# An even beat of loads, later weights and re-ordered row transposes in a gated linear attention followed by domain-routed experts

## The chip, the core and the metric

The kernel runs on one NeuronCore of a Trainium2 chip, in one launch. The metric is the device time of one execution in microseconds (us). TensorE does the matrix products, VectorE and ScalarE the elementwise work, GpSimd issues the indirect transfers and the weight loads, SyncE issues the loads of the inputs. Sixteen DMA engines serve all of them.

## The reference

Two parts, one after the other. The first is a recurrence over 768 time steps for 4 batches and 8 heads of 48 channels, with a complex decay per channel:

```python
mag = np.sqrt(a_re*a_re + a_im*a_im)
scale = np.minimum(mag, 0.999) / (mag + 1e-06)
a_re_n, a_im_n = a_re*scale, a_im*scale
for t in range(S):
    new_re = ar*S_re - ai*S_im
    new_im = ar*S_im + ai*S_re
    S_re, S_im = new_re + einsum('bhd,bhe->bhde', k[:,:,t], v[:,:,t]), new_im
    y[:,:,t] = einsum('bhd,bhde->bhe', q[:,:,t], S_re)
```

The second takes each of the 3072 tokens (4 x 768 rows of 384 numbers) through the one of 8 experts that its `domain_id` names:

```python
h = np.maximum(x[mask] @ w1[e], 0.0)     # 384 -> 1024
out[mask] = h @ w2[e]                    # 1024 -> 384
```

## The kernel before, in words

**Attention.** Each batch is cut into 6 chunks of 128 time steps, so there are 24 chunks, numbered g, and each chunk is worked in two halves of four heads: 48 steps, numbered s, step 2g and 2g+1 for chunk g. The decays of a batch are turned into logarithms and angles (`le_a`, `le_b`, `trig_a`), summed over time by matrix products with triangular masks (`sums`, L329), and made into factors by ScalarE (`le_c` writes the tile em, `trig_b` the tile sc). `prods(g)` (L344) multiplies k and q of chunk g into em on VectorE, `cat(g)` (L370) multiplies the sines and cosines in. Then `transposes(s)` (L382, copies L386 and L388), `scores(s)` (L394, masked on VectorE in L396), `state(g)` (L408), and `outputs(s)` (L422, L424), which writes rows of 384 numbers through the tile xst to a DRAM buffer for each batch, `gl_x_rows`.

**Experts.** `routing()` works out for each batch and expert which rows belong to it (up to 128), as lists of row numbers inv_sb. Each of the 32 pairs of batch and expert is one expert step: `gather` (L434, an indirect load of 128 rows of `gl_x_rows`, issued by GpSimd three steps ahead), `ffn_a` (three row transposes on TensorE, L442, and a copy on VectorE, L444), `ffn_b` (24 products and two ReLU copies, L456 and L458), `ffn_c` (8 products, a copy and an indirect store, L465 to L468). xt_ps of `ffn_a` and o_ps of `ffn_c` share one PSUM bank.

**Order.** The head prepares batch 0 and runs `routing`. Then a loop over s calls in each step `scores(s)`, the loads placed at this step, `outputs(s - 2)`, `transposes(s + 2)`, `state`, the preparation of the following batch (placed by `add`), and `expert_step(s)`. A framework then orders the instructions of each engine: it plays the program through with its own model of durations, and takes the earlier-written instruction where several are ready. So an instruction can come ahead of earlier-written ones on its engine if the model thinks that its inputs are there; a manual dependency (`add_manual_dep` with `nosync`) forbids that for a pair.

**Loads.** All input loads are one chain on SyncE's queue (`sp`, L122): the decays (576 KB each), k and q (two of 192 KB in one of six kq buffers) and v (192 KB in one of four vf buffers, cast to bf16 by `cast_v`, L119, at step 2g-3). One that waits for its buffer holds all behind it. The weights are 40 pieces, five for each expert, issued by GpSimd (L276, L279), each gated by the masking of the step at which `w_place(n)` puts it. An expert step is planned at the first free step that is three behind its last weight piece and at least 6 behind the end of its batch; steps 44 to 47 take none. What does not fit runs after step 47. Worked out from these formulas, before: weights end at step 35, expert steps are 18 to 20, 25, 29 to 40, 42, 43 and 48 to 61, so 14 of 32 lie behind the attention steps.

Of the kernel before, what the change touches and what calls it, by code (L numbers as in the profile page):

```python
# [25 lines left out]
NCH = S // TC  # L26
# [22 lines left out]
def kernel(  # L49
# [56 lines left out]
    def load_kq(g, which):  # L106
        if which == 0:
            kq_t[g] = lpool.tile([128, 2, H, D], F32, name="kq", bufs=6)
        sp(out=kq_t[g][:, which], in_=chunk_view((k, q)[which], g))
# [1 line left out]
    vf_t = {}  # L111

    def load_v(g):
        vf_t[g] = lpool.tile([128, H, D], F32, name="vf", bufs=4)
        sp(out=vf_t[g][:, :, :], in_=chunk_view(v, g))

    def cast_v(g):
# [14 lines left out]
    for g in range(NCH):  # L132
        load_kq(g, 0)
        load_kq(g, 1)
        if g < 4:
            load_v(g)


    def const(name, dt, val=1.0, cols=128):
# [202 lines left out]
    def prods(g):  # L342
        t = em[g // 2][:, :, g % 2]
        nc.vector.tensor_tensor(out=t, in0=kq_t[g][:, :, :, :].rearrange("p a h d -> p a (h d)"), in1=t, op=ALU.mult)  # L344
# [32 lines left out]
    def transposes(s):  # L377
# [10 lines left out]
        eng(out=flat(qt), in_=t_ps[0:96, 1].rearrange("p h t -> p (h t)"))  # L388
        kts[s], qts[s] = kt, qt

    def scores(s):
        s_ps = bank([128, 4, TC], F32, "s_ps", "s")
        for h in range(4):
            nc.tensor.matmul(out=s_ps[:, h, :], lhsT=kts[s][:, h, :], rhs=qts[s][:, h, :], start=True, stop=True)  # L394
        m = epool.tile([128, 4, TC], BF16, name="mtm", bufs=3)
        i = nc.vector.tensor_tensor(out=m[:, :, :], in0=s_ps[:, :, :],  # L396
                                    in1=mask[:, None, :].to_broadcast([128, 4, TC]), op=ALU.mult)
        mtms[s] = m
        return i
# [39 lines left out]
    def ffn_a(x):  # L439
        xt_ps = bank([128, 3, 128], F16, "xt_ps", "x")  # L440
        for fs in range(3):
            nc.tensor.transpose(out=xt_ps[:, fs, :], in_=x[:, fs * 128:(fs + 1) * 128], identity=ident16[:, :])  # L442
        xt = mpool.tile([128, 3, 128], F16, name="xt", bufs=2)
        nc.vector.tensor_copy(out=xt[:, :, :], in_=xt_ps[:, :, :])  # L444
        return xt
# [27 lines left out]

    def w_place(n):

        return n if n < 12 else 12 + (n - 12) * 3 // 2 if n < 20 else 24 + (n - 20) * 3 // 5

    preload = lambda name: chain("act", nc.scalar.preload_act_table_set(name))  # L478

# [3 lines left out]
    def add(s, f):  # L483
        steps[s].append(f)

    for b in range(1, B):
        s0 = 12 * (b - 1)
        g0 = b * NCH
        A, Z = (b, 0), (b, 1)
        add(s0 + 0, lambda: preload(SET_LE))  # L490
        add(s0 + 0, lambda A=A: le_a(A))
        add(s0 + 1, lambda Z=Z: le_a(Z))
        add(s0 + 1, lambda A=A: le_b(A))
        add(s0 + 2, lambda Z=Z: le_b(Z))
        for n, s in ((0, 2), (1, 3), (2, 4)):
            add(s0 + s, lambda p=g0 // 2 + n: le_c(p))
            add(s0 + s, lambda g=g0 + 2 * n: prods(g))
            add(s0 + s + 1, lambda g=g0 + 2 * n + 1: prods(g))
        add(s0 + 5, lambda: preload(SET_TRIG))
        add(s0 + 6, lambda A=A: trig_a(A))  # L500
        add(s0 + 6, lambda Z=Z: trig_a(Z))
        for n, s in ((0, 6), (1, 8), (2, 10)):
            add(s0 + s, lambda p=g0 // 2 + n: trig_b(p))

    for g in range(3, B * NCH):
        add(2 * g - 5, lambda g=g: cat(g))

    loads = {s: [] for s in range(NS)}
    for b in range(2, B):
        s0 = 12 * (b - 2)  # L510
        for hf in range(NH):
            loads[s0 + 3].append(lambda b=b, hf=hf: load_decay(b, hf, 0))
            loads[s0 + 7].append(lambda b=b, hf=hf: load_decay(b, hf, 1))
        for n in range(NCH):
            for w in range(2):
                loads[s0 + (3, 4, 5, 5, 8, 8)[n]].append(lambda g=b * NCH + n, w=w: load_kq(g, w))
    for g in range(6, B * NCH):
        loads[2 * g - 10].insert(0, lambda g=g: load_v(g))
    for g in range(3, B * NCH):
        add(2 * g - 3, lambda g=g: cast_v(g))  # L520

# [7 lines left out]
    left = [(b, e) for b in range(B) for e in range(NE)]  # L529
    s = 0  # L530
    while left:
        ready = [(b, e) for b, e in left if s >= 12 * (b + 1) + 6 and s >= w_slot[e] + WLAT]
        if ready and not NS - 4 <= s < NS:
            plan[s] = ready[0]
            left.remove(ready[0])
        s += 1
# [10 lines left out]
        load_decay(1, hf, 0)  # L547
    for n in range(3):
        le_c(n, (None, ("s", "x"), ("y", "h"))[n])
        prods(2 * n)  # L550
        prods(2 * n + 1)
        if n < 2:
            for g in range(2):
                load_kq(NCH + 2 * n + g, 0)
                load_kq(NCH + 2 * n + g, 1)
        if n == 0:
            routing()
    preload(SET_TRIG)
    trig_a(A)
    for g in range(3):  # L560
        cast_v(g)
    for g in range(4, 6):
        load_v(g)
    trig_a(Z)
    for hf in range(NH):
        load_decay(1, hf, 1)
    for g in range(4, 6):
        load_kq(NCH + g, 0)
        load_kq(NCH + g, 1)
    trig_b(0)  # L570
    cat(0)
    transposes(0)
# [2 lines left out]
    trig_b(1, ("x", "h"))  # L575
    cat(2)
    trig_b(2)
    xrows, xts, hs = {}, {}, {}
    order = [plan[s] for s in sorted(plan)]
    GA = 3  # L580
# [35 lines left out]
    def overflow():  # L616
        count = nc.values_load(ovf_i[0:1, 0:1], min_val=0, max_val=S)
        with tc.If(count > CAP):
# [5 lines left out]
            for b in range(B):  # L624
                with tc.For_i(0, NE, 1) as e:
# [8 lines left out]
                    for c in range(OVC):  # L634
                        ffn_c(ffn_b(ffn_a(gather(b, c, invo[:, c, 1:2])), w1o), w2o, invo[:, c, 0:1])

    overflow()


# [28 lines left out]
```

## Time and profile before

| what | us |
|---|---|
| median of 3 runs | 282.45 |
| lowest and highest run | 281.96 and 285.29 |
| profiled execution, its time | 280.33 |
| its span in the trace | 278.7 |
| TensorE busy in it | 211.2 (76%) |
| VectorE busy | 178.6 (64%) |
| ScalarE busy | 176.0 (63%) |
| GpSimd busy | 99.9 (36%) |

The trace covers the span; the time beside it has 1.6 us more around it. A busy share is an average over the whole span, and the stretches differ much, so the views below go by stretches.

### The profile page before, as it was taken

What the parts mean: (1) busy time and instruction counts of PE and PEld (TensorE: products, weight loads), DVE (VectorE), ACT (ScalarE), POOL (GpSimd) and SP (SyncE); (2) the same over time, 40 slices, a digit from 0 to 9 for tenths busy, and PEclk for the clock granted to TensorE, in tenths of its full rate; (3) what the DMA queues carried; (4) which work ended last, traced back from release to release, by engine and by line L of the source; (5) the groups of instructions that cost most, each with busy time, mean ns of one, the idle gap of its engine ahead of it and who ended that gap; (6) DMA issues with size and microseconds to landing.
All of it is one profiled execution on the core that took longest, in us unless ns stands there. A gap on an engine that the chain in (4) does not pass through costs nothing.

```text
span 278.7 us, 6242 instructions
## 1 busy us (share of the span) xinstructions
PE 211.2 (76%) x2450; PEld 164.3 (59%) x2450; DVE 178.6 (64%) x371; ACT 176.0 (63%) x264; POOL 99.9 (36%) x129
## 2 busy tenths in 40 slices
PE   0064766595872678899648999999889898999990
PEld 0032356474562576677537777677668677787760
DVE  4599998989796498899959988473435361111100
ACT  4769259957556588686994696655344545554650
POOL 8000003011102710125584476453634244666322
PEclk9999866669695559999975999999999999999997
DMA  7999999999999989999999989773221211222111
GB/s 188 251 187 173 260 173 260 217 270 235 218 242 244 199 138 257 208 245 247 220 217 227 195 162 229 161 140 90 66 67 66 60 69 50 87 62 81 60 52 50
DMA packets 104405, 46.13 MB, mean 166 GB/s; under 512 B 77745, under 2 KB 97711, under 8 KB 104368
## 3 DMA queue, kind: packets, MB, share of 16 engines
q1 hardware_dynamic: 91520, 23.60, 42.2%
q0 software_dynamic: 9392, 19.70, 33.3%
q10 hardware_dynamic: 3456, 2.36, 2.7%
q8 instruction: 21, 0.34, 0.6%
q14 instruction: 16, 0.13, 0.1%
HBM read 51.93 MB, written 8.65 MB: 217 GB/s over the span
## 4 chain that ended last, share of the span: by engine, by line
PE 38%; DVE 17%; ACT 15%; DMA 14%; issue 10%; POOL 3%; another core or an unknown queue 1%; SPq 1%; ACTq 0%; POOLq 0%; DVEq 0%
PE h_ps L456 10%; PE cum L329 9%; PE o_ps L465 8%; DMA vf<-in_v_dram 5%; PE t_ps L382 4%; ACT em L338 4%; POOL out_dram L468 3%; DMA gl_x_rows<-xst 3%; DMA dom_i<-in_moe_domain_id_dram 2%; DVE em L344 2%; DMA kq<-in_k_dram 2%; DVE cat L370 2%; PE xt_ps L442 2%; ACT L478 2%; DVE fg L357 2%
## 5 line engine op out<-in xcount | busy, mean ns | idle before, releaser
L458 ACT ACTIVATE h_sb<-h_ps 128x512 f16<-128x512 f32 x64 | 37.9, 597 | 32.4 <-PE h_ps L456 20.4
L468 POOL DMA_INDIRECT out_dram<-o_sb,inv_sb x32 | 33.3, 1041 | 51.8 <-ACT o_sb L467 42.3
L456 PE MATMUL h_ps<-xt,w1t 128*128 128x128 f16 x672 | 47.2, 221 | 3.2 <-ACT h_sb L458 2.0
L382 PE MATMUL t_ps<-ident,cat 128*96 128x128 bf16 x384 | 37.2, 248 | 16.0 <-DVE qt L388 9.4
L456 PEld LDWEIGHTS <-w1t 128*128 128x128 f16 x672 | 42.7, 114 | 8.5 <-issue 6.7
L434 POOL DMA_INDIRECT xrow<-gl_x_rows,inv_sb x32 | 38.0, 1186 | 26.2 <-DMA kq<-in_k_dram 8.9
L465 PE MATMUL o_ps<-w2t,h_sb 128*128 128x384 f16 x224 | 43.1, 326 | 2.1 <-DVE xt L444 1.3
L382 PEld LDWEIGHTS <-cat 128*96 128x96 bf16 x384 | 31.7, 144 | 20.5 <-DVE qt L388 10.9
L396 DVE TENSOR_TENSOR mtm<-s_ps,mask 128x512 bf16<-128x512 f32 x48 | 32.8, 682 | 13.3 <-PE s_ps L394 11.8
L276 POOL DMA_DIRECT2D w1t<-in_moe_w_dram x21 | 11.6, 558 | 81.4 <-DVE mtm L396 59.9
L386 DVE COPY kt<-t_ps 96x512 bf16<-96x512 bf16 x48 | 20.0, 416 | 19.5 <-PE t_ps L382 19.2
L444 DVE COPY xt<-xt_ps 128x384 f16<-128x384 f16 x32 | 11.3, 352 | 32.1 <-PE xt_ps L442 27.7
L465 PEld LDWEIGHTS <-h_sb 128*128 128x128 f16 x256 | 23.5, 98 | 14.1 <-issue 2.2
L329 PEld LDWEIGHTS <-upto 128*128 128x128 f16 x144 | 15.6, 111 | 20.7 <-issue 14.6
L370 DVE TENSOR_TENSOR cat<-em,sc 128x768 bf16<-128x768 bf16 x48 | 25.6, 549 | 1.4 <-PE h_ps L456 0.8
L344 DVE TENSOR_TENSOR em<-kq,em 128x768 bf16<-128x768 f32 x24 | 22.0, 952 | 3.6 <-ACT em L338 3.6
L394 PE MATMUL s_ps<-qt,kt 96*128 96x128 bf16 x192 | 22.8, 247 | 0.8 <-DVE mtm L396 0.7
L329 PE MATMUL cum<-lm,upto 128*128 128x384 f16 x72 | 18.6, 396 | 4.9 <-DVE lm L312 4.4
L467 ACT COPY o_sb<-o_ps 128x384 f32<-128x384 f32 x32 | 15.3, 477 | 10.2 <-PE o_ps L465 7.8
L329 PE MATMUL cum<-th,upto 128*128 128x384 f16 x72 | 17.4, 366 | 4.1 <-ACT th L348 3.7
L338 ACT ACTIVATE em<-cum,bias_m 128x768 bf16<-128x768 f32 (+1 forms) x14 | 11.3, 810 | 13.8 <-PE cum L329 13.7
L422 PE MATMUL y<-v,mtm 128*128 128x48 bf16 x192 | 17.8, 194 | 2.3 <-DVE mtm L396 1.9
(88 smaller groups left out, 374.0 us busy)
## 6 DMA issues: line engine op xcount, KB each, us to landing
w1t<-in_moe_w_dram POOLq DMA_DIRECT2D x21, 256.0 KB
w2t<-in_moe_w_dram POOLq DMA_DIRECT2D x14, 384.0 KB
dec_sb<-in_a_re_dram SPq DMA_DIRECT2D x8, 576.0 KB
dec_sb<-in_a_im_dram SPq DMA_DIRECT2D x8, 576.0 KB
kq<-in_k_dram SPq DMA_DIRECT2D x24, 192.0 KB
kq<-in_q_dram SPq DMA_DIRECT2D x24, 192.0 KB
vf<-in_v_dram SPq DMA_DIRECT2D x24, 192.0 KB
gl_x_rows<-xst ACTq DMA_DIRECT2D x24, 96.0 KB
```

Of the source, the lines that this page charges most:

```text
L329: nc.tensor.matmul(out=o, lhsT=m[:, :], rhs=t[:, :, j * D:(j + 1) * D], start=(i == 0), stop=(i == len(mm) - 1))
L338: chain("act", nc.scalar.activation(out=t[:, n, k], in_=ps, func=AF.Exp, scale=sgn, bias=bias[:, 0:1]))
L344: nc.vector.tensor_tensor(out=t, in0=kq_t[g][:, :, :, :].rearrange("p a h d -> p a (h d)"), in1=t, op=ALU.mult)
L370: nc.vector.tensor_tensor(out=t[:, :, :, part, :], in0=e.rearrange("p a (h d) -> p a h d", h=H), in1=sc[:, part].rearrange("p (h d) -> p h ...
L382: nc.tensor.transpose(out=t_ps[0:96, a, h, :], in_=cats[g][:, a, hf * 4 + h].rearrange("p a d -> p (a d)"), identity=ident[:, :])
L394: nc.tensor.matmul(out=s_ps[:, h, :], lhsT=kts[s][:, h, :], rhs=qts[s][:, h, :], start=True, stop=True)
L396: i = nc.vector.tensor_tensor(out=m[:, :, :], in0=s_ps[:, :, :], in1=mask[:, None, :].to_broadcast([128, 4, TC]), op=ALU.mult)
L434: nc.gpsimd.indirect_dma_start(out=x[:, :], out_offset=None, in_=x_ap[b][:, :], in_offset=bass.IndirectOffsetOnAxis(ap=idx, axis=0), bound ...
L456: nc.tensor.matmul(out=h_ps[:, jj, :], lhsT=cols[:, fs, blk, jb], rhs=xt[:, fs, :], start=(fs == 0), stop=(fs == 2))
L458: nc.scalar.activation(out=h_sb[:, a * 4:a * 4 + 4, :].rearrange("p j t -> p (j t)"), in_=h_ps[:, :, :].rearrange("p a t -> p (a t)"), fun ...
L465: nc.tensor.matmul(out=o_ps[:, :], lhsT=h_sb[:, j, :], rhs=w2[:, j, :], start=(j == 0), stop=(j == 7))
L468: ins = nc.gpsimd.indirect_dma_start(out=out[:, :], out_offset=bass.IndirectOffsetOnAxis(ap=inv, axis=0), in_=o_sb[:, :], in_offset=None, ...
```

## The change

Loads: v gets six buffers; in the head all six v chunks of batch 0 are loaded beside k and q. From then on v(g) is loaded at step 2g-13 and k, q of chunk g at step 2g-17 (before, k and q of a batch came in a bunch at its steps 3 to 8 of the batch two ahead, v(g) at 2g-10). `prods(g)` moves to step 2g-6, for the last three chunks of batch 0 too, which leaves three of them in the head. Weights: two pieces in three steps for the first 16, then four in three steps, ending at step 41. Expert steps come at the earliest 7 behind a batch. By the formulas the expert steps are then 19, 20, 24, 29, 31 to 38, 40, 41, 43 and 48 to 64: 17 of 32 lie behind the attention steps. Row transposes of `ffn_a` are ordered behind the last `scores` written ahead of them. `routing()` stands last in the head.

```diff
-        vf_t[g] = lpool.tile([128, H, D], F32, name="vf", bufs=4)
+        vf_t[g] = lpool.tile([128, H, D], F32, name="vf", bufs=6)
...
-        if g < 4:
-            load_v(g)
+        load_v(g)
...
+    pe_mark = [None]
...
-            nc.tensor.matmul(out=s_ps[:, h, :], lhsT=kts[s][:, h, :], rhs=qts[s][:, h, :], start=True, stop=True)
+            pe_mark[0] = nc.tensor.matmul(out=s_ps[:, h, :], lhsT=kts[s][:, h, :], rhs=qts[s][:, h, :],
+                                          start=True, stop=True)
...
-            nc.tensor.transpose(out=xt_ps[:, fs, :], in_=x[:, fs * 128:(fs + 1) * 128], identity=ident16[:, :])
+            i = nc.tensor.transpose(out=xt_ps[:, fs, :], in_=x[:, fs * 128:(fs + 1) * 128], identity=ident16[:, :])
+            if pe_mark[0] is not None:
+                tc.add_manual_dep(i.ins, pe_mark[0].ins.name, nosync, reason="order")
...
-        return n if n < 12 else 12 + (n - 12) * 3 // 2 if n < 20 else 24 + (n - 20) * 3 // 5
+        return n * 3 // 2 if n < 16 else 24 + (n - 16) * 3 // 4
...
-            add(s0 + s, lambda g=g0 + 2 * n: prods(g))
-            add(s0 + s + 1, lambda g=g0 + 2 * n + 1: prods(g))
...
+        add(2 * g - 6, lambda g=g: prods(g))
         add(2 * g - 5, lambda g=g: cat(g))
...
-        for n in range(NCH):
-            for w in range(2):
-                loads[s0 + (3, 4, 5, 5, 8, 8)[n]].append(lambda g=b * NCH + n, w=w: load_kq(g, w))
     for g in range(6, B * NCH):
-        loads[2 * g - 10].insert(0, lambda g=g: load_v(g))
+        loads[max(0, 2 * g - 13)].append(lambda g=g: load_v(g))
+        for w in range(2 if g > 8 else 0):
+            loads[max(0, 2 * g - 17)].append(lambda g=g, w=w: load_kq(g, w))
...
-        ready = [(b, e) for b, e in left if s >= 12 * (b + 1) + 6 and s >= w_slot[e] + WLAT]
+        ready = [(b, e) for b, e in left if s >= 12 * (b + 1) + 7 and s >= w_slot[e] + WLAT]
...
-        prods(2 * n)
-        prods(2 * n + 1)
-        if n < 2:
-            for g in range(2):
-                load_kq(NCH + 2 * n + g, 0)
-                load_kq(NCH + 2 * n + g, 1)
-        if n == 0:
-            routing()
+        for g in ((0, 1), (2,), ())[n]:
+            prods(g)
+            load_kq(NCH + g, 0)
+            load_kq(NCH + g, 1)
...
-    for g in range(4, 6):
-        load_v(g)
...
-    for g in range(4, 6):
-        load_kq(NCH + g, 0)
-        load_kq(NCH + g, 1)
...
     trig_b(2)
+    routing()
...
+    pe_mark[0] = None
     overflow()
```

## Rows read from the trace of the kernel before

**Rows 1.** The page: TensorE's busy line, and DMA share in 40 slices
```profile
PE 211.2 (76%) x2450; PEld 164.3 (59%) x2450; DVE 178.6 (64%) x371; ACT 176.0 (63%) x264; POOL 99.9 (36%) x129
...
DMA  7999999999999989999999989773221211222111
```

**Rows 2.** Stretches: length, busy us of PE, PEld, DVE, ACT, POOL; clock, DMA share, GB/s
```profile
41.00:86.40 45.40, 33.24 (x334) 25.89 (x334) 40.73 (x73) 33.49 (x44) 6.48 (x12) 0.73 1.12 244
93.00:142.80 49.80, 41.62 (x494) 33.52 (x495) 45.47 (x82) 40.87 (x56) 17.59 (x20) 0.88 1.06 216
...
151.80:187.40 35.60, 33.68 (x430) 26.73 (x428) 27.55 (x52) 26.32 (x43) 19.02 (x23) 0.98 0.89 182
187.40:228.80 41.40, 36.66 (x523) 29.98 (x519) 18.80 (x43) 20.16 (x41) 17.25 (x18) 1.00 0.23 71
228.80:276.00 47.20, 41.45 (x503) 32.70 (x502) 5.35 (x14) 23.12 (x43) 24.01 (x24) 1.00 0.21 67
```

**Rows 3.** VectorE in order of time, L396: steps 0, 29, 36 and 47
```profile
41.29 0.68 DVE L396 TENSOR_TENSOR mtm<-s_ps,mask 128x512 bf16<-128x512 f32 x1
...
151.78 0.69 DVE L396 TENSOR_TENSOR mtm<-s_ps,mask 128x512 bf16<-128x512 f32 x1 [0.27 <-PE y L424]
...
187.42 0.68 DVE L396 TENSOR_TENSOR mtm<-s_ps,mask 128x512 bf16<-128x512 f32 x1
...
228.83 0.69 DVE L396 TENSOR_TENSOR mtm<-s_ps,mask 128x512 bf16<-128x512 f32 x1
```

**Rows 4.** All engines in order of time, 84 to 95: start, length, in brackets idle before
```profile
88.73 1.23 POOL L434 DMA_INDIRECT xrow<-gl_x_rows,inv_sb  x1 [6.96 <-DMA kq<-in_k_dram]
...
93.07 0.50 PE L442 MATMUL xt_ps<-ident,xrow 128*128 128x128 f16 x3 [6.60 <-DMA xrow<-gl_x_rows,inv_sb]
...
93.56 1.07 PE L382 MATMUL t_ps<-ident,cat 128*96 128x128 bf16 x8
93.77 0.48 ACT L428 CAST xst<-y 128x384 f16<-128x384 f32 x1 [5.44 <-issue]
...
94.66 0.42 DVE L386 COPY kt<-t_ps 96x512 bf16<-96x512 bf16 x1 [5.67 <-PE t_ps L382]
```

**Rows 5.** All engines in order of time, 132 to 148
```profile
132.71 14.06 SPq L122 DMA_DIRECT2D vf<-in_v_dram  x5
...
134.59 1.72 POOL L276 DMA_DIRECT2D w1t<-in_moe_w_dram  x3 [1.11 <-DVE xt L444]
...
136.36 0.61 PE L382 MATMUL t_ps<-ident,cat 128*96 128x128 bf16 x8 [0.55 <-ACT qt L388]
...
146.02 0.36 DVE L119 CAST v<-vf 128x384 bf16<-128x384 f32 x1 [3.13 <-DMA vf<-in_v_dram]
...
147.09 1.09 PE L382 MATMUL t_ps<-ident,cat 128*96 128x128 bf16 x8 [2.23 <-DVE qt L388]
```

**Rows 6.** SyncE's queue: what its issues waited for: us, times, longest
```profile
SPq L122 <- DVE kt L386: 22.6, 7, 13.0
```

**Rows 7.** VectorE groups, 7 to 41: count, busy us, mean ns
```profile
L344 DVE TENSOR_TENSOR em<-kq,em 128x768 bf16<-128x768 f32 x6 | 5.6, 947 | 0.0
L230 DVE TENSOR_TENSOR at<-r,rank 128x768 f16<-128x768 f16 x4 | 3.6, 949 | 0.0
```

**Rows 8.** VectorE in time: first and last of routing (40), last of prods (24)
```profile
7.87 0.18 DVE L199 CAST fb<-dom_i 128x24 f32<-128x24 int32 x1 [3.93 <-DMA dom_i<-in_moe_domain_id_dram]
...
28.63 0.17 DVE L251 CAST dest_i<-fb 128x24 int32<-128x24 f32 x1
...
160.89 1.83 DVE L344 TENSOR_TENSOR em<-kq,em 128x768 bf16<-128x768 f32 x2 [0.59 <-ACT em L338]
```

**Rows 9.** VectorE in time, behind the steps: first full and last expert pitches
```profile
231.61 0.36 DVE L444 COPY xt<-xt_ps 128x384 f16<-128x384 f16 x1 [1.38 <-PE h_ps L456]
...
262.27 0.36 DVE L444 COPY xt<-xt_ps 128x384 f16<-128x384 f16 x1 [2.45 <-PE xt_ps L442]
265.08 0.36 DVE L444 COPY xt<-xt_ps 128x384 f16<-128x384 f16 x1 [2.45 <-PE xt_ps L442]
```

## The prediction, as it stood before the run

> **What bounds the kernel now.** I began with the busy lines and the row of DMA shares [rows 1]: no engine is busy for the whole span, and the DMA engines are full up to about 190 us and at a fifth behind that. So the program has to be read by stretches. The starts of the masking instructions say where the steps lie [rows 3]: the loop begins at 41.3, step 29 at 151.8, step 36 at 187.4, the last step at 228.8. The table of stretches [rows 2] then shows three regimes.
>
> From 41 to about 152 VectorE sets the pace. It is busy 40.7 of 45.4 us (90%) ahead of 86.4 and 45.5 of 49.8 us (91%) between 93 and 142.8, while TensorE has 73% and 84% at a mean clock of 0.73 and 0.88 of full. From 151.8 TensorE sets it: 33.7 of 35.6 us (95%), 36.7 of 41.4 (89%), 41.5 of 47.2 (88%), at full clock, and VectorE falls to 45% and below after 187. The DMA share is above 1 in the first regime, so transfers are a second candidate there.
>
> The table leaves out two holes on purpose. In the first [rows 4] TensorE is idle for 6.60 us up to 93.07, waiting for the gathered rows of the first expert step; behind that row transpose stand, in its queue, the output products whose copy ScalarE waits for (5.44 us idle) and the transposes that VectorE waits for (5.67 us idle). This is step 14, while `ffn_a` for this expert step was written into step 17: the framework moved it ahead. In the second [rows 5] VectorE is idle for 3.13 us before a cast, waiting for a v chunk; the copies behind the cast hold TensorE for 2.23 us. SyncE was working through five v loads for 14.06 us and three weight pieces went out at 134.59, so the chunk was late in a crowd.
>
> **The change part by part, against the profiled execution's 280.33 us.**
>
> *Row transposes behind scores; expert steps 7 behind a batch.* The first expert step is planned at 19, its rows are transposed behind the scores of step 18, and the last rows of batch 0 are still written by the outputs placed in step 13. That is five steps later than their source, at (151.8 - 41.3) / 29 = 3.8 us a step some 19 us. The gather was issued at 88.73 and used at 93.07, 4.3 us. The hole goes. All three engines stand still in it; VectorE is what bounds this stretch, so I take its 5.67 us. What is late next is VectorE itself. The dependency adds no semaphore; queued behind it are only the copy L444 and the products of one expert step, which have a whole step.
>
> *v three steps earlier, six buffers, k and q eleven steps ahead of `prods`.* A v chunk is issued at 2g-13 and cast at 2g-3: ten steps, 38 us. Its buffer came free at 2g-15, that of k and q one step before the load, so a load no longer stands in SyncE's queue before a full buffer, as it does now (22.6 us in seven waits of one kind alone, [rows 6]). Value: the 3.13 us of the second hole. Bounds: 0, if the chunk is late because all transfers are, to 3.13.
>
> *Weights.* Up to step 29 the pace before issues 30 pieces, the new one 24, and the ten of steps 24 to 29 become eight. That supports the line above and gets no value of its own. Its price: by the plans, 28 expert steps are left from step 29 on before and 29 after. Where VectorE bounds the steps an expert step is hidden, where TensorE bounds them it costs its pitch. The pitch behind the steps is 2.81 us at the end [rows 9], and (265.08 - 231.61) / 11 = 3.04 over all; I take 2.9. So +2.9.
>
> *`prods`.* One costs 0.95 us of VectorE [rows 7]. Three leave the head, 2.8 us; but the same three come in steps 0 to 4. Before, 18 of 24 had run by step 29, the other six from 153 to 162.7 [rows 8]; after, 18 are placed by then too. So in the stretch where VectorE bounds, nothing is gained. At the late end the last three go to steps 36 to 40, where VectorE has room, from a stretch with TensorE at 95%: between 0 and -2.8; I take -1.
>
> *Routing last in the head.* Forty VectorE instructions from 7.87 to 28.63 [rows 8], the four largest 3.6 us together [rows 7]. The gather needs them only at step 16. Their work is conserved and fills VectorE's gaps in the head or goes between the first steps; the state product of step 0 needs the same PSUM bank. Bounds: -3 (the angles of batch 0 come earlier by what stood before them) to +4 (they stand in a chain between head and step 0). I take 0, since VectorE is full on either side. In SyncE's queue the first decays of batch 1 now stand behind two v loads more, the second ones behind one pair of k and q fewer: 0.
>
> *Clock.* The granted clock falls to 1.2 GHz of 2.4 after the holes: eight transposes take 1.07 and 1.09 us behind them and 0.61 shortly before the second [rows 4, 5], 0.46 us more for a step. With some six such steps, an estimate from the two mean clocks of the first regime, that is 2.8 us of TensorE time, while VectorE bounds: 0 to -3, I take -1.
>
> Sum: -5.7 - 3.1 + 2.9 - 1 - 1 = -7.9 us, 272.4 for the profiled execution. That one was 2.1 us below the median of the runs shown, so the forecast against the median is 282.45 - 7.9 = **274.5 us**, 2.8% less. About 2% is what a measurement of this kernel can tell from no change, 5.6 us.
>
> **A rule against it.** "DMA: Bandwidth & Descriptors" of the Trainium skill, section "Issuing engines are not separate DMA queues", says that transfers issued from any engine run on the same 16 DMA engines and interleave there, so that who issues them saves only issue time. The full shares of this trace up to 190 us agree with it. By that rule the same bytes in another order take the same time, and the first rival follows.
>
> **The rivals.** *Transfers bound the first 150 us.* The bytes are unchanged and the share is above 1 from 41 to 142.8 [rows 2]. Then the second hole closes at one place and opens at another, VectorE's slack of 9% is transfer time too, and the clock follows: only the first hole goes. -5.7 + 2.9 = -2.8: 279.6, no difference that can be told. Against it speaks that VectorE at 90% leaves little to wait for, and that k and q now have 38 us to land.
>
> *Late weights push experts out and the steps don't shrink: slower.* Behind the last step stand 17 expert steps instead of 14: 3 x 2.9 = 8.7 us more at the end. In my forecast the steps from 29 on give back all but 2.9 of it, because TensorE bounds them. In the stretch 187 to 229, though, TensorE is at 89%, and a step also is a chain of transposes, copies, scores and masking; if this chain is the bound there, an expert step that is taken out shortens nothing. It decides when step 47 doesn't begin at least 8.7 us sooner than 228.8. With the first hole's 5.7 lost to transfers too, as in the rival above, the end is 282.45 + 8.7 = 291.2; with it gained, 285.5.
>
> *More than the sum.* If the clock stays up and the head gives its 2.8 us: -5.7 - 3.1 + 2.9 - 3 - 2.8 - 1 = -12.7: 269.8.
>
> *It doesn't do what it says.* The framework may order the engines otherwise, and only the row transposes are tied. Without the tie's effect the hole stays, and the one more hidden expert is lost: about 285. The dependency makes this unlikely.
>
> **How the numbers follow.** Chances: forecast 0.50, transfers bound 0.20, more than the sum 0.10, slower by late weights 0.16, not as said 0.04. The range reaches from the rich case with both holes at their full price, 267, to beyond the transfers case and the first unknown cost of +4 on it, 283. That leaves out the late weights, the fifth case and a part of the rich one, 0.21. Faster by over 2% (under 276.8) is the rich case and most of the forecast, 0.52; within 2% are the transfers case, the rest of the forecast, the fifth case and a third of the late weights, 0.37; slower (over 288.1) the rest of the late weights, 0.11.
>
> **What would show it.** Right: no idle time of several us on TensorE before a row transpose in the first half; the first L444 copy behind the masking of step 18; no cast that waits for a v load; SyncE's waits for full buffers gone; step 29 some 9 us sooner, near 143; 17 copies L444 behind the last masking at the same 2.8 to 3 us; the DMA share lower before step 29 and stretched to beyond step 41. Wrong: a product of an expert that waits for a weight load, a `prods` that waits for k or q, step 0 later than 41.3, because routing stands before it, or a last step that begins near 220 or later.

## The result, and the profile after

The changed kernel takes 280.5 us (median of 20 runs, 276.89 to 283.57) beside 282.98 us for the kernel before on the same chip; the ratio is 0.987, 95% interval 0.984 to 0.990. It isn't the quotient of these medians (0.991), because every ratio here is formed from the fast runs of a kernel, without those over 1.5% above its fastest; the profiles of e9, e16, e17 and the first of the changed kernel are of such slower runs. The ratio means about 3.6 us less (0.0128 x 282.45) where 7.9 less was forecast, and less than the 2% that count as a difference here.

The first profile of the changed kernel is of an execution of 283.57 us, the longest of its 20. Both kernels were therefore profiled once more, unchanged (the runs e1_after_again and e5_before_again below: 271.49 and 274.42 us, spans 269.9 and 272.8). These two are compared here; the chips differ, with 277.02 and 275.98 us for the kernel before. In the changed kernel's lines the mask is L398, `prods` L343, the copy of transposed rows L448 and the v cast still L119.

Stretches between the masks of steps 0, 12, 18, 29, 36 and 47, and from there to the end of expert work; the columns are those of [rows 2], and the edges are rounded to 0.1 us. First the kernel before, in its second profile:

```profile
41.50:85.00 43.50, 32.24 (x316) 24.95 (x315) 38.85 (x69) 31.51 (x43) 6.46 (x12) 0.70 1.09 236
85.00:111.30 26.30, 16.23 (x181) 14.50 (x181) 18.47 (x35) 18.59 (x25) 7.49 (x9) 0.61 1.02 205
111.30:152.20 40.90, 32.60 (x382) 24.72 (x383) 36.12 (x67) 31.15 (x44) 20.91 (x21) 0.93 1.13 227
152.20:186.90 34.70, 33.38 (x431) 26.80 (x429) 27.23 (x53) 26.10 (x43) 19.23 (x23) 0.98 0.91 187
186.90:224.00 37.10, 36.34 (x531) 30.10 (x527) 18.48 (x44) 20.32 (x41) 17.64 (x18) 1.00 0.26 81
224.00:268.00 44.00, 40.73 (x501) 32.32 (x497) 5.26 (x14) 23.59 (x43) 22.91 (x24) 1.00 0.20 65
```

The same stretches of the changed kernel, second profile:

```profile
39.70:82.50 42.80, 30.24 (x334) 23.90 (x333) 39.21 (x73) 32.10 (x44) 4.35 (x8) 0.77 1.03 220
82.50:103.70 21.20, 16.28 (x143) 13.16 (x144) 18.00 (x33) 16.46 (x21) 11.82 (x8) 0.52 1.01 219
103.70:142.90 39.20, 32.41 (x395) 25.56 (x393) 36.54 (x68) 31.44 (x45) 15.76 (x18) 0.89 1.11 225
142.90:177.40 34.50, 30.45 (x388) 24.39 (x387) 26.93 (x52) 24.72 (x40) 15.74 (x18) 0.98 0.88 171
177.40:211.40 34.00, 33.07 (x489) 27.60 (x485) 18.07 (x41) 18.67 (x38) 19.93 (x23) 1.00 0.72 152
211.40:265.00 53.60, 49.58 (x611) 39.52 (x608) 6.71 (x18) 28.64 (x52) 29.72 (x30) 1.00 0.21 68
```

Read the first two columns downwards. Step 0 comes 1.8 us sooner, steps 0 to 12 give 0.7, steps 12 to 18 give 5.1 and steps 18 to 29 give 1.7: step 29 begins at 142.9 instead of 152.2, 9.3 us sooner, as forecast (near 143). Then the gain stops growing: steps 29 to 36 take 34.5 us instead of 34.7, although TensorE has 2.9 us less to do in them. From the last mask to the last copy of rows it is 44.5 us instead of 35.0. The last copy comes at 255.90 instead of 259.02: 3.1 us are left of 9.3.

Both holes of [rows 4, 5] recur in the second profile of the kernel before (all engines in order of time; the bracket is the idle time ahead of the instruction and what ended it):

```profile
94.03 0.50 PE L442 MATMUL xt_ps<-ident,xrow 128*128 128x128 f16 x3 [7.22 <-DMA xrow<-gl_x_rows,inv_sb]
...
146.30 0.36 DVE L119 CAST v<-vf 128x384 bf16<-128x384 f32 x1 [2.76 <-DMA vf<-in_v_dram]
```

In the changed kernel, in the same view, the first transposes of gathered rows come behind the scores of step 18 without a bracket, and their copy behind the mask of that step:

```profile
102.82 0.63 PE L395 MATMUL s_ps<-qt,kt 96*128 96x128 bf16 x4
103.25 0.49 PE L444 MATMUL xt_ps<-ident,xrow 128*128 128x128 f16 x3
...
103.73 0.68 DVE L398 TENSOR_TENSOR mtm<-s_ps,mask 128x512 bf16<-128x512 f32 x1
...
104.33 0.34 DVE L448 COPY xt<-xt_ps 128x384 f16<-128x384 f16 x1
```

No v cast waits for its chunk any more. The line of [rows 6], 22.6 us in the first profile of the kernel before, goes from the first of these lines (kernel before, second profile) to the second (changed kernel, second profile):

```profile
SPq L122 <- DVE kt L386: 17.7, 3, 13.0
```

```profile
SPq L122 <- DVE kt L385: 5.4, 3, 3.6
```

SyncE's waits are not gone, though: by all lines of that view its load issues waited 78.3 us before and 53.4 after. The engine named is only the one that came last, so the view doesn't tell which of them were waits for a full buffer.

What is new stands in VectorE's order behind the mask of step 29 (142.91), changed kernel, second profile:

```profile
142.91 0.69 DVE L398 TENSOR_TENSOR mtm<-s_ps,mask 128x512 bf16<-128x512 f32 x1
...
145.12 0.95 DVE L343 TENSOR_TENSOR em<-kq,em 128x768 bf16<-128x768 f32 x1
...
148.30 0.95 DVE L343 TENSOR_TENSOR em<-kq,em 128x768 bf16<-128x768 f32 x1
...
149.50 1.81 DVE L343 TENSOR_TENSOR em<-kq,em 128x768 bf16<-128x768 f32 x2
...
153.71 0.94 DVE L343 TENSOR_TENSOR em<-kq,em 128x768 bf16<-128x768 f32 x1
157.49 0.96 DVE L343 TENSOR_TENSOR em<-kq,em 128x768 bf16<-128x768 f32 x1 [2.85 <-DMA kq<-in_q_dram]
158.37 0.68 DVE L398 TENSOR_TENSOR mtm<-s_ps,mask 128x512 bf16<-128x512 f32 x1
```

These are the last six products (18 to 23), all ahead of the mask of step 32. The program writes them into steps 30 to 40. The last pair of k and q is loaded at step 29, and SyncE, in the order of its queue, issues it here:

```profile
147.12 1.13 SPq L122 DMA_DIRECT2D kq<-in_k_dram  x1
148.29 2.69 SPq L122 DMA_DIRECT2D kq<-in_q_dram  x1
```

So the pair that was to have eleven steps to land was wanted 3.7 us after its issue ended (154.65 against 150.98), and VectorE stood for 2.85 us with the mask of step 32 queued behind. In the first profile, of 283.57 us, the same product waited 5.54 us, up to 160.38.

### The profile page after: what moved, and what is told of

Its sections match the earlier page's. It is cut to its first block, busy times and chain, and to the rows that moved or that the text cites. A ratio compares the mean times of both kernels' runs of the same rounds, so it can differ in the third digit from the quotient of the medians.

```text
span 282.0 us, 6241 instructions
## 1 busy us (share of the span) xinstructions
PE 212.2 (75%) x2450; PEld 165.1 (59%) x2450; DVE 177.8 (63%) x371; ACT 176.1 (62%) x264; POOL 105.5 (37%) x129
## 4 chain that ended last, share of the span: by engine, by line
PE 36%; DVE 25%; ACT 13%; DMA 9%; issue 8%; SPq 4%; POOL 3%; POOLq 0%; DVEq 0%; ACTq 0%
PE h_ps L460 11%; PE o_ps L469 10%; DMA kq<-in_q_dram 6%; PE cum L328 5%; PE t_ps L381 4%; SPq L122 4%; DVE mtm L398 3%; DVE cat L369 3%; POOL out_dram L472 3%; DVE lm L309 3%; DVE fg L356 3%; ACT em L337 3%; DVE dec_sb L298 2%; DMA dom_i<-in_moe_domain_id_dram 2%; DVE fg L357 2%
## 5 line engine op out<-in xcount | busy, mean ns | idle before, releaser
L436 POOL DMA_INDIRECT xrow<-gl_x_rows,inv_sb x32 | 43.6, 1362 | 20.0 <-PE h_ps L460 5.1
L381 PE MATMUL t_ps<-ident,cat 128*96 128x128 bf16 x384 | 37.9, 246 | 15.7 <-ACT qt L387 10.6
L460 PE MATMUL h_ps<-xt,w1t 128*128 128x128 f16 x672 | 46.3, 221 | 2.8 <-ACT h_sb L462 2.2
L460 PEld LDWEIGHTS <-w1t 128*128 128x128 f16 x672 | 42.1, 114 | 6.4 <-issue 4.6
L275 POOL DMA_DIRECT2D w1t<-in_moe_w_dram x21 | 12.1, 577 | 75.0 <-DVE mtm L398 37.0
L448 DVE COPY xt<-xt_ps 128x384 f16<-128x384 f16 x32 | 11.3, 354 | 44.7 <-PE xt_ps L444 21.2
L398 DVE TENSOR_TENSOR mtm<-s_ps,mask 128x512 bf16<-128x512 f32 x48 | 32.7, 681 | 10.6 <-PE s_ps L395 10.6
L469 PEld LDWEIGHTS <-h_sb 128*128 128x128 f16 x256 | 23.7, 99 | 14.3 <-issue 3.0
L343 DVE TENSOR_TENSOR em<-kq,em 128x768 bf16<-128x768 f32 x24 | 22.5, 947 | 7.5 <-DMA kq<-in_q_dram 7.5
L328 PE MATMUL cum<-lm,upto 128*128 128x384 f16 x72 | 17.8, 382 | 7.2 <-DVE lm L311 6.4
L424 PE MATMUL y<-v,mtm 128*128 128x48 bf16 x192 | 16.8, 192 | 6.1 <-DVE mtm L398 5.4
L395 PEld LDWEIGHTS <-kt 96*128 96x128 bf16 x192 | 15.9, 111 | 7.6 <-issue 6.5
L328 PE MATMUL cum<-th,upto 128*128 128x384 f16 x72 | 19.8, 407 | 0.7 <-ACT th L347 0.5
```

What stands on the lines that cost most here:

```text
L328: nc.tensor.matmul(out=o, lhsT=m[:, :], rhs=t[:, :, j * D:(j + 1) * D], start=(i == 0), stop=(i == len(mm) - 1))
L381: nc.tensor.transpose(out=t_ps[0:96, a, h, :], in_=cats[g][:, a, hf * 4 + h].rearrange("p a d -> p (a d)"), identity=ident[:, :])
L395: pe_mark[0] = nc.tensor.matmul(out=s_ps[:, h, :], lhsT=kts[s][:, h, :], rhs=qts[s][:, h, :], start=True, stop=True)
L436: nc.gpsimd.indirect_dma_start(out=x[:, :], out_offset=None, in_=x_ap[b][:, :], in_offset=bass.IndirectOffsetOnAxis(ap=idx, axis=0), bound ...
L460: nc.tensor.matmul(out=h_ps[:, jj, :], lhsT=cols[:, fs, blk, jb], rhs=xt[:, fs, :], start=(fs == 0), stop=(fs == 2))
L469: nc.tensor.matmul(out=o_ps[:, :], lhsT=h_sb[:, j, :], rhs=w2[:, j, :], start=(j == 0), stop=(j == 7))
```

## The experiments

The theory after the result, *products ahead of their loads*: the framework moves the products ahead of their written steps (as it moved `ffn_a` in the kernel before), so the loads no longer lead them, VectorE waits for q in steps 29 to 32, and what the experts give back is lost there. The rivals: *transfers bound*, theory D of the expectations (the bytes take their time, a hole that closes opens elsewhere), *late weights*, theory B (the experts pushed to the end cost it), and, formed later, *ScalarE's row writes*, theory E (the writes of finished rows, which ScalarE issues, hold it up behind the input loads). Ratios are to the kernel before, run in turn on the same chip, with the 95% interval. The chips differ (274.9 to 285.4 us for the kernel before), so only ratios are compared between groups.

**The two kernels once more.** e1_after_again is the changed kernel, e5_before_again the kernel before, both without an edit.

> The changed kernel once more, for a second profile. Theory A (new holes: the framework moves the products of k and q with the factors up to nine steps ahead of where they are written, so that they wait for late k and q): the idle time of VectorE before them, 7.5 us in the first profile, is there again within 3 us, and the time is 278 to 282 us. Theory B (the price is only in the 17 expert steps behind the attention steps): the holes before the products were an accident of that execution and are under 2 us here, and the time is the same.

> The kernel before, for a second profile. Its holes depend on when loads land. Theory A (the two holes read from the first profile are worth 8.8 us of the time): both are there again, 5 to 7 us before the first row transpose and some 3 us before a cast. Theory C (holes of the first profile were partly an accident of that execution, so that a sum over it promises too much): the two together are under 6 us here.

The changed kernel repeats: 0.987 (0.978 to 0.997). Its products wait 4.1 us for q in all, beside 7.5 us in the first profile: less than the 4.5 that theory A asked for, more than the 2 of its rival. e5_before_again was for its profile alone. The split by stretch above is that of this pair.

**The products tied to their steps.** e3_pin puts every product on VectorE behind the mask of the step in which it is written:

```
     def prods(g):
-        nc.vector.tensor_tensor(out=t, ...)
+        i = nc.vector.tensor_tensor(out=t, ...)
+        if mask_mark[0] is not None:
+            tc.add_manual_dep(i.ins, mask_mark[0].ins.name, nosync, reason="order")
...
         mtms[s] = m
+        mask_mark[0] = i
```

> The changed kernel with one addition: the products of k and q with the factors are tied on VectorE behind the masking of the step at which they are written, so that the lead of eleven steps is real. Theory A: no VectorE wait for k or q is left, and the time falls by 4 to 7 us against the changed kernel, to 274 to 276 us. Theory B: the wait is not what the time hangs on; within 2 us of the changed kernel, 278 to 282 us.

It took 0.982 (0.974 to 0.990), 270.33 us beside 271.06 of the changed kernel on the same chip. The wait is gone. VectorE from step 29 on; its mask is L401 here:

```profile
144.34 0.68 DVE L401 TENSOR_TENSOR mtm<-s_ps,mask 128x512 bf16<-128x512 f32 x1
...
147.64 0.95 DVE L343 TENSOR_TENSOR em<-kq,em 128x768 bf16<-128x768 f32 x1
...
157.94 0.68 DVE L401 TENSOR_TENSOR mtm<-s_ps,mask 128x512 bf16<-128x512 f32 x1
...
162.11 0.94 DVE L343 TENSOR_TENSOR em<-kq,em 128x768 bf16<-128x768 f32 x1
```

One product stands between the masks of steps 29 and 32 where there were six, and none waits. Steps 29 to 36 take 30.9 us instead of 34.5. The end is 2.2 us earlier in the profiles (last copy at 253.74), not 3.6, since step 29 begins 1.4 us later (144.3); by the medians it is 0.7, which these runs alone can't tell from nothing. The wait went as theory A said, but the time did not fall by its 4 to 7 us; 0.7 lies with the rival's "within 2 us".

**One part undone.** Each of these is the changed kernel with one part as before: e4_no_tie without the dependency of the row transposes, e6_old_weights with the old pace of weights (15 experts instead of 17 behind the last mask), e7_old_loads with the old loads, four value buffers and `prods` at the old places, e8_routing_first with `routing()` early in the head.

```
e4  -            if pe_mark[0] is not None:
    -                tc.add_manual_dep(i.ins, pe_mark[0].ins.name, nosync, reason="order")
e6  -        return n * 3 // 2 if n < 16 else 24 + (n - 16) * 3 // 4
    +        return n if n < 12 else 12 + (n - 12) * 3 // 2 if n < 20 else 24 + (n - 20) * 3 // 5
e7  the hunks of load_v, prods, load_kq and the head taken back
e8  +        if n == 0:
    +            routing()
    ...
    -    routing()
```

> The changed kernel without the order of row transposes behind scores. Theory A: the first row transposes come ahead again and TensorE waits some 6 us for gathered rows: 4 to 7 us slower than the changed kernel, 284 to 287 us. Rival: the expert steps that start one step later than before suffice: within 2 us of the changed kernel.

> The changed kernel with the weights at the places of before; 15 instead of 17 expert steps lie behind the attention steps. Theory B (late weights push expert steps out and the steps do not shrink): two expert steps fewer at the end, 4 to 6 us under the changed kernel, a ratio to the kernel before of 0.965 to 0.975. Theory A (TensorE bounds the late steps, so that an expert step costs the same in either place): within 2 us of the changed kernel, a ratio of 0.98 to 0.995.

> The changed kernel with the loads of k, q and v, their products with the factors and the four buffers for v as before; order of row transposes, weights and routing as changed. Theory A: the hole before a cast comes back, and the products no longer wait for k or q: within 3 us of the kernel before, a ratio of 0.99 to 1.01. If the beat of loads is worth nothing: the ratio of the changed kernel, 0.98 to 0.99.

> The changed kernel with the routing in its old place, behind the first products of the head. Forecast of the study (0, with bounds from -3 to +4): within 2 us of the changed kernel. If the routing's place held up the angles of batch 0: 2 to 4 us slower than the changed kernel, with step 0 beginning later by that much.

Measured: e4 0.997 (0.992 to 1.002), e6 1.006 (1.002 to 1.011), e7 0.990 (0.986 to 0.994), e8 0.989 (0.979 to 0.998). Where routing stands makes no difference, as forecast: step 0 begins at 39.6 in e8, at 39.7 in the changed kernel. Without the tie a hole of 3.75 us stands on TensorE before the first row transposes (to 91.87), and the gain is gone: 0.997 beside 0.987, a smaller loss than the 4 to 7 us expected. Without the new loads a cast waits again, but no product does. VectorE's waits in e7:

```profile
DVE v L119 <- DMA vf<-in_v_dram: 4.2, 1, 4.2
```

In e7's profile step 29 begins 5.3 us later than in the changed kernel (148.2), and steps 29 to 36 then take 3.5 us less (31.0). By the ratios, 0.990 beside 0.987, the new loads with their products gain nothing that these runs can tell: in these profiles, what they give up to step 29 is mostly lost again behind it.

The surprise is e6. The pace of the weights had been given no value of its own; with the old pace the change gains nothing. VectorE's waits say why:

```profile
DVE em L343 <- DMA kq<-in_q_dram: 11.4, 3, 5.7
```

The 11.4 us are at 113.52 (5.30), at 163.72 (5.71) and one short wait: products that run ahead meet q loads that land late. That they land late because by the old pace 30 pieces of weights instead of 24 are placed up to step 29 is argued, not shown.

**One part alone.** e2_tie_only is the kernel before with the dependency of the row transposes and nothing else, e10_new_weights_only with the new `w_place` and nothing else.

> The kernel before with nothing of the change but the row transposes of the experts ordered behind the last scores written ahead of them. Theory A: the hole of 5.7 to 6.6 us before the first row transpose goes and nothing comes in its place: 277 to 279 us, 4 to 6 us under the kernel before. Rival (transfers bound the first 150 us): the wait moves to a load, a gain of under 2 us: 281 us or more.

> The kernel before with the new pace of weights alone (expert steps planned by the old rule from it). Theory D: most of the change's gain, a ratio of 0.985 to 0.995, although the first row transposes still come ahead. Theory A (the gain is in the order of row transposes and in the beat of loads): no gain, 1.00 to 1.02, for three expert steps more lie behind the attention steps.

e2 took 1.013 (1.006 to 1.019): slower than before, although its hole is gone and step 18 begins at 107.2 instead of 111.3. Nine us further on, VectorE waits for a v chunk:

```profile
116.32 0.36 DVE L119 CAST v<-vf 128x384 bf16<-128x384 f32 x1 [4.84 <-DMA vf<-in_v_dram]
```

Step 29 begins at 153.6, later than before. e10 took 0.991 (0.987 to 0.995), as *transfers bound* expected, and no v cast in its profile waits longer than 0.2 us. Alone, then, the part to which the forecast gave 5.7 us gains nothing, and the one that it gave none gains 0.9%. With the old loads and the old weights, closing the hole only brings VectorE to the next chunk sooner: for this combination *transfers bound* was right.

**Weights early, then late.** e9_pin_old_weights is e3 with the old pace of weights, e11_pin_fast_late is e3 with pieces two a step from step 24 on (15 experts behind the last mask), e12_old_issue_new_plan is the changed kernel with weights issued at the old places and experts planned as by the new ones.

```
e11 -        return n * 3 // 2 if n < 16 else 24 + (n - 16) * 3 // 4
    +        return n * 3 // 2 if n < 16 else 24 + (n - 16) // 2
e12 -        s = w_place(n)
    +        s = n if n < 12 else 12 + (n - 12) * 3 // 2 if n < 20 else 24 + (n - 20) * 3 // 5
    -        w_slot[e] = s
    +        w_slot[e] = w_place(n)
```

> The changed kernel with the old pace of weights and with the products of k and q tied behind the masking of their step. If the old pace hurts only because the products are taken ahead and meet late loads (Theory A): 0.97 to 0.985, as with the tie and the new pace, or better, since two expert steps fewer lie at the end. If transfers as such bound the first 150 us (Theory D): another wait takes its place, 0.995 or more.

> The changed kernel with the products of k and q tied, and with the weights at the new pace up to step 24 and two pieces a step from there, ending at step 35; 15 expert steps lie behind the attention steps. With the lead of eleven steps real, the loads of steps 24 to 29 have slack: 2 to 5 us under the tie alone, a ratio of 0.965 to 0.978. If transfers bound up to step 36: within 2 us of the tie alone, 0.978 to 0.99.

> The changed kernel with the weight pieces issued at the places of before, and the expert steps planned as in the changed kernel, 17 of them behind the attention steps. Theory D (transfers bound the first 150 us, and the change gains by taking weight pieces out of them): as slow as with both, a ratio to the kernel before of 1.00 or more, with VectorE waiting 8 us or more for k, q or v. Rival (the plan of the expert steps did it): the ratio of the changed kernel, 0.98 to 0.99.

e9 0.979 (0.971 to 0.987); e11 1.018 (1.012 to 1.023); e12 1.019 (1.015 to 1.024). e9 against e6 is the clearest effect of the tie: the same weights, 2.7% apart, intervals that don't meet. So the old pace costs something only while products run ahead of their loads. e11 has no wait for k or q on VectorE either and is still slow, which neither of its expectations had. There ScalarE stood behind writes of finished rows for 3.5 us ahead of step 29 and for 6.2 us behind it, and in e12 for 6.3, with the idle time put down to input loads that neither instruction reads. ScalarE in e12 in order of time:

```profile
156.88 0.33 ACTq L431 DMA_DIRECT2D gl_x_rows<-xst  x1
157.25 0.47 ACT L413 CAST wst<-w_ps 96x384 bf16<-96x384 f32 x1 [6.30 <-DMA vf<-in_v_dram]
```

What the write waits for stands in the semaphores of the traces, the counters on which the instructions of a program wait for a transfer. In this program SyncE's loads and ScalarE's row writes take the same eight of them in turn. Just ahead of each of these writes ScalarE has an instruction that waits for the counter which the write is to use, and its last user was a load: the v load issued at 135.83 in e12 (counter 114), and in e11 a v load (108) and a q load (116). So the write waits for that load to land because the program has it so, and ScalarE's work behind it waits along.

**Row writes by GpSimd.** If these waits are what costs the time, the writes should leave ScalarE's queue. Four kernels with that one edit: e13 the changed kernel, e14 with e3's tie, e15 of e11, e16 of e12.

```
-            nc.scalar.dma_start(out=x_ap[b][c * TC:(c + 1) * TC, :], in_=xst[:, :])
+            nc.gpsimd.dma_start(out=x_ap[b][c * TC:(c + 1) * TC, :], in_=xst[:, :])
```

> The changed kernel with the rows of the attention written by GpSimd's queue instead of ScalarE's. Theory E (the row write waits on the completion of an input load eight transfers back, since both share eight completion counters, and holds ScalarE): 3 to 5 us under the changed kernel, a ratio to the kernel before of 0.97 to 0.98. Theory D (only the transfers count): within 2 us of the changed kernel, or slower by GpSimd's queue.

> The same with the products of k and q tied behind the masking of their step. Theory E: both kinds of waits are gone, a ratio of 0.965 to 0.98, under the tie alone (0.982).

> The tied kernel with two weight pieces a step from step 24, which was 1.0175 of the kernel before, with the rows written by GpSimd's queue. Theory E: its two holes of ScalarE (4.2 and 6.2 us between a row copy and its write) go, a ratio of 0.965 to 0.985. Theory D: the crowd of loads and weights around 150 us is what costs, a ratio of 1.00 or more.

> The changed kernel with the weights issued at the old places and the new plan of expert steps, which was 1.019 of the kernel before, with the rows written by GpSimd's queue. Theory E: the hole of ScalarE of 6.4 us goes, a ratio of 0.985 to 1.00, what is left being the waits for k and q. Theory D: 1.01 or more.

e13 1.017 (1.011 to 1.023), e14 1.003 (0.998 to 1.007), e15 1.006 (1.000 to 1.012), e16 1.027 (1.020 to 1.034). The waits for loads go, but as a remedy the theory fell: e13 and e14 are slower than the kernels without the edit (0.987 and 0.982), and e16 is no faster than e12. GpSimd's queue in e13 shows the price, two lines of its waits:

```profile
POOL gl_x_rows L431 <- ACT xst L430: 28.7, 10, 5.6
...
POOL xrow L436 <- DMA gl_x_rows<-xst: 9.0, 3, 3.4
```

The writes wait for ScalarE's copies at the head of the queue in which the weights and gathers stand. Only in e15 did the edit help (1.018 to 1.006, intervals that just touch; steps 29 to 36 from 37.6 to 29.4 us). "DMA: Bandwidth & Descriptors" of the Trainium skill, section "Issuing engines are not separate DMA queues", says that starting transfers from several engines saves only the sequencer's time to initiate them. Here it mattered more who issues 24 writes: the ratio moved up by 0.030 (e1 to e13) and 0.021 (e3 to e14) and down by 0.012 (e11 to e15). The waits above suggest that this comes from what stands behind a write in its engine's queue, of which that sentence doesn't treat. e13 and e14, on one chip, are the second test of the tie: 1.017 to 1.003, and again the intervals don't meet.

**The best version.** e17_best_again is e9 once more, e18_after_beside the changed kernel on the same chip.

> The changed kernel with the products of k and q tied and the old places of weights once more, beside the changed kernel on one chip. If the tie takes away what the change lost behind step 29: no VectorE wait for k or q, step 29 to step 36 in 31 to 33 us, and a ratio to the kernel before of 0.97 to 0.985, under that of the changed kernel. If the earlier 0.979 was luck of that chip: within 0.3% of the changed kernel.

> The changed kernel a third time, on the same chip as the one above: a ratio of 0.984 to 0.992, VectorE waiting 3 to 8 us for k or q, and step 29 to step 36 in 31 us plus that part of the wait which lies between them.

e17 0.980 (0.973 to 0.987), 268.8 us; e18 0.987 (0.982 to 0.991), 271.66; the kernel before 275.97. The changed kernel with the products tied and the old pace of weights is the fastest here, 2% below the kernel before in two measurements; beside the changed kernel it leads by 2.9 us of medians, with intervals that overlap. No product waits for k or q, but its profiled execution, the longest of its seven, missed the expected 31 to 33 us for steps 29 to 36 (41.1, by a wait of ScalarE, shown in the last section).

**All profiles in one table.** Steps 29 to 36 hold six copies of expert rows in each of these kernels. The third column is the idle time in that stretch which the trace puts down to an input load or its issue: VectorE's before a product, or ScalarE's behind a row write (s); two shorter ones of ScalarE, 1.43 us in e1 and 1.68 in e8, are left out. The second terms of e13 and e16 are put down to another instruction of SyncE's queue (L612); that they too are waits for a q load is argued, because the product reads a q tile whose load SyncE had just issued. The last column is the difference.

```
kernel      29 to 36   wait        rest
e15         29.4       0           29.4
e14         30.2       0           30.2
e3          30.9       0           30.9
e7          31.0       0           31.0
e9          31.9       0           31.9
e4          32.9       1.85        31.1
e8          34.3       2.11        32.2
e1          34.5       2.85        31.7
changed, 1st 37.1      5.54        31.6
e18         37.4       4.71        32.7
e11         37.6       6.24 (s)    31.4
e6          38.0       5.71        32.3
e13         39.9       4.58+3.46   31.9
e17         41.1       10.70 (s)   30.4
e12         41.5       6.30 (s)    35.2
e16         43.8       9.29+2.33   32.2
```

The length runs over 14.4 us and the rest, e12 aside, over 3.3. Without e9, e16, e17 and the changed kernel's first profile it is 12.1 and the same 3.3; without the two argued terms the rest of e13 is 35.4 and that of e16 34.5. The expected length with one expert step fewer than before is 34.7 - 2.9 = 31.8. So the steps shrank by about what was forecast, and the waits for loads came on top. No run speaks against this reading of one execution each, but e12's 3.4 us over it stay unexplained. It covers this stretch alone: steps 36 to 47 take 34.0 us in e1 and e3 and between 36.4 and 42.9 in e14, e6, e17, e11, e15 and e9, which hold five to seven copies of expert rows there.

## Why the prediction was right and wrong

*Row transposes behind scores, -5.7.* Steps 12 to 18, which hold the hole, gave 5.1. Right in place and size within the whole change. e2 shows that it isn't a value of this edit alone: what was late next was not "VectorE itself" but a v chunk.

*v and the second hole, -3.1.* Steps 18 to 29 gave 1.7. No v cast waits; the sign to look for came, at about half the price. e7 undoes this part together with `prods`: -4.1 was forecast for the two, and without them the ratio is 0.990 beside 0.987.

*The head, 0.* That "the same three come in steps 0 to 4" and nothing is gained by it was wrong on the good side: the products ahead of step 0 went from the first line (kernel before, second profile) to the second (changed kernel),

```profile
L344 DVE TENSOR_TENSOR em<-kq,em 128x768 bf16<-128x768 f32 x6 | 5.6, 954 | 0.0
```

```profile
L343 DVE TENSOR_TENSOR em<-kq,em 128x768 bf16<-128x768 f32 x4 | 3.6, 943 | 0.0
```

step 0 began 1.8 us sooner, and steps 0 to 12 took 0.7 less all the same. In e7, with six again, step 0 begins at 41.7. *Clock, -1:* the granted clock rose in steps 0 to 12 (0.70 to 0.77) and fell in 12 to 18 (0.61 to 0.52) and 18 to 29 (0.93 to 0.89); no gain can be made out. Up to step 29 the terms make -9.8 and -9.3 was measured, partly by errors that cancel.

*One more expert step behind step 29, +2.9.* By the copies L448, steps 29 to 36 hold six instead of seven and all behind them 22 instead of 20: -2.9 and +5.8 by the forecast's price. Behind step 36 it was +6.4 (-3.1 to the last mask, +9.5 behind it), and the experts follow each other at 2.80 us. Changed kernel, second profile, VectorE:

```profile
253.10 0.36 DVE L448 COPY xt<-xt_ps 128x384 f16<-128x384 f16 x1 [2.45 <-PE xt_ps L444]
255.90 0.36 DVE L448 COPY xt<-xt_ps 128x384 f16<-128x384 f16 x1 [2.45 <-PE xt_ps L444]
```

The price held. Between steps 29 and 36 the 2.9 came as -0.2.

*`prods`, -1: the step that failed.* "At the late end the last three go to steps 36 to 40, where VectorE has room" took the written places for the places in the engine's order, and "k and q now have 38 us to land" the written lead for the real one. The products ran before step 32, the last one 3.7 us after its q load had been issued, and instead of giving 1 us the edit cost 2.7: the 2.85 us wait. That is 3.7 of the 4.8 us between the forecast (-7.9) and this pair of profiles (-3.1); the rest is 0.5 up to step 29 and 0.6 behind step 36. The forecast had the clue: it had read in [rows 4] that `ffn_a` was moved three steps ahead of its place, and it named "a `prods` that waits for k or q" among the signs of an error, but gave it no price and no case. That the wait makes the steps long is shown by e3 (wait gone, 30.9 us), and that such waits cost time over the whole run by the two ties e6 to e9 and e13 to e14, in kernels with other weights or other row writes. That it is the whole of the shortfall is not shown: with the products tied, e3 gains 1.8% and e17 2.0%, about 5 to 5.7 us of 282.45, not 7.9, and e3 by itself can't be told from the changed kernel. What keeps the other 2 to 3 us is open.

*Weights, "no value of its own".* Wrong as long as products run ahead: e6 against the changed kernel. With products tied it holds (e3 0.982, e9 0.979).

*Routing, 0.* Right (e8). *The range.* Its lower end, 267, does not follow from the terms; the richest case adds up to 269.8.

*The rivals.* "Transfers bound the first 150 us" failed for the whole change (step 29 came 9.3 us sooner at a DMA share of 1.01 to 1.11) and held for the tie alone (e2); the waits behind step 29 are its mechanism in another place, at a share of 0.88. It gave 279.6, nearest to the result, but by losing the second hole and not by what happened. "Late weights" fell by its own test: step 47 began 12.6 us sooner (10.0 in the first profiles) where 8.7 were asked for, and e6, with two experts fewer behind the last mask, is slower.

Open: why e2 loses more than its one wait, why e9, e11 and e15 stay long in steps 36 to 47 (42.9, 42.0 and 42.7 us), e12's rest, and how often the wait for q has which length; the profiles give one execution each.

## What to carry to other kernels

A lead in steps between a load and its use counts only if the use stays where it is written: before pricing loads "n steps ahead", look in the trace of before whether the engine's order follows the written order, and tie the use if it doesn't. Read a gain at each later stage: here 9.3 us were there at step 29 and a third of them at the end. And parts of one change need not add up: the tie of the transposes alone made the kernel slower, and the pace of the weights was worth 2% or nothing, depending on where the products stood.

## What the runs showed of the hardware

An engine can stand for a transfer that it neither issued nor reads, when it shares completion counters with it. In e17's profile (an execution of 279.07 us, where its runs have a median of 268.8) SyncE's load issues take long:

```profile
145.32 7.55 SPq L122 DMA_DIRECT2D kq<-in_q_dram  x1
152.96 11.43 SPq L122 DMA_DIRECT2D vf<-in_v_dram  x1
```

and ScalarE's row write, whose rows were ready at 158.3, goes out at 169.11; the activation behind it waited 10.70 us, though its own input is on chip. The write was given counter 116, whose last user was the q load of 145.32; ScalarE waited until that load had landed, 23.7 us after its issue, as in e11 and e12 above:

```profile
158.16 0.62 ACT L466 ACTIVATE h_sb<-h_ps 128x512 f16<-128x512 f32 x1
169.11 0.33 ACTq L435 DMA_DIRECT2D gl_x_rows<-xst  x1
169.48 0.60 ACT L466 ACTIVATE h_sb<-h_ps 128x512 f16<-128x512 f32 x1 [10.70 <-DMA kq<-in_q_dram]
```

The issue of the same 192 KB load took from 0.70 to 7.55 us for q and 0.93 to 11.43 us for v within 30 us of this execution. And executions of one kernel spread by 4% on one chip (the kernel before, 273.36 to 284.45 us on e1's); what makes that spread is not shown.
